# Row-chain stages and weight handling in the half passes of an interleaved convolution and MLP kernel: which is issued first in a step

## The chip, the cores and the metric

The kernel runs on one core of a Trainium2 chip. The metric is the device time of one execution of the whole program, in microseconds. The core's engines each work through a queue of their own: TensorE (PE, matmuls and transposes), VectorE (DVE), ScalarE (ACT), GpSimd (POOL) and SyncE (SP), which here issues the DMAs. An instruction that waits holds back all that stand behind it on its engine.

## The reference

Four layers, in turn of kind A and of kind B, on x of 2048 tokens (S) by 1024 channels (D), in fp32:

```
def A(q, k, v):                       # H3 convolution layer
    k_shift = causal depthwise conv of k, 4 taps
    kv = k_shift * v
    y = long causal depthwise conv of kv with ssm_k (2048 taps, by FFT) + kv * ssm_D
    return q * y
def B(x):                             # MLP, F = 3584
    h = x @ w1 + b1
    h = max(h, 0) ** 2
    return h @ w2 + b2
x = A_q
x = x + A(layernorm(x), A_k, A_v)
x = x + B(layernorm(x))
x = x + A(layernorm(x), A_k, A_v)
x = x + B(layernorm(x))
```

## The kernel before

**Tiling.** The tokens are cut into 4 blocks of 512, each of 4 tiles of 128. The MLP of one layer on one block is a unit; there are eight, in the order `ORDER = [(0,0), (1,0), (0,1), (0,2), (0,3), (1,1), (1,3), (1,2)]` (MLP layer, block). The fifth and sixth, and the seventh and eighth, are computed jointly and are not touched here. An fp32 product is made of three matmuls on split operands (`mm3`, L391 to L394): high by high, high by low, low by high. The convolution is computed by matmuls, too, and its work is spread between the steps of the MLP.

**Steps.** A unit is a list of steps. A step "m1" multiplies one 128 x 512 piece of w1 with the block's transposed, split rows (`xh`, `xl`), and adds into a PSUM bank; two such steps make 128 hidden channels, and `relu2` (L1627, L1628, L1630 on ACT, L1635 on DVE) follows. A step "m2" multiplies by a piece of w2. Mostly a step works on all 512 tokens. In a half pass it works on tiles 0 and 1 alone, or on 2 and 3 (128 x 256 matmuls). There are half passes in "m1" at the start of the first unit (4 groups of hidden channels, two steps each, on each half) and at the start of the second unit (6 groups: 12 half steps on tiles 0 and 1, then 12 on 2 and 3); the steps of the latter stand behind the last "m2" steps of the first unit, since both units work on block 0. Half steps of kind "m1" have the phase "x".

**Row chain.** Between the first two units the rows of block 0 go through the convolution layer of the second pair: the MLP result is added (`evict1`, L1737), normalised, multiplied by the convolution's y and added to the residual (`rows`, L1730 on ACT; L1720, L1722, L1724 on DVE), normalised again (L1763 on ACT, L1765 on DVE), transposed on PE (L1774) and split into `xh` (L1782 on ACT) and `xl` (L1783 on DVE). It runs on two tiles at a time, in eleven stages; the reciprocal square root is a row of short DVE instructions (L809 to L813). The stages of tiles 2 and 3 run under the half steps on tiles 0 and 1 of the second unit. Each stage has a due step, counted from the end of the half in question (the table `CHAIN`, L93); when a step comes, all stages due are issued. Other work waits in the same list (`lag`) for its due step: `relu2`, the loads of the residual rows (`load_acc`, L1796, four of 512 KB), the broadcast load of b2 (`load_b2`, L1801, 512 KB into a `px` tile) and its additions on POOL (`add_b2`, L1805). Two shorter lists, `soon` and `behind`, are emptied ahead of and behind it.

**Weights.** `w_advance(s, w)` (L1161) moves three pointers ahead of step s with weight w. It loads a raw 256 KB piece up to 9 weights ahead into one of eight `wr` rows (L1129, L1132); casts it to a high half in a `whl` or `jr` buffer (L1142, on ACT); and subtracts to make the low half (L1150). A piece that was split before can be stored (`w_store`, L1158, to a DRAM tile `wd_m...`) and loaded again later as a pair of 512 KB (L1138), which needs neither cast nor subtraction. In phase "x" the low halves go to POOL three times of four and else to DVE (`WLO`), and the pointers for cast and low half run one and two weights farther.

**Order within a step.** The loop issues `soon`, then `lag` and `w_advance` (in phase "x" `w_advance` first, else `lag` first), then `behind`, then the step's matmuls. It decides only the order within each engine's queue; semaphores do the rest.

Of the kernel before, what the change touches and what calls it, by code (L numbers as in the profile page):

```python
# [297 lines left out]
def tile_h3_mlp(ctx: ExitStack, tc: tile.TileContext, q, kT, vT, shk, ssmT, ssmD, w1, b1, w2, b2,  # L298
# [735 lines left out]
    phase = [""]  # L1034
# [27 lines left out]
    def from_pair(w):  # L1062
        return w not in single and split_kept(wsrc[w]) and w - first_w.get(wsrc[w], w) >= PAIR_GAP
# [4 lines left out]
    def room(w):  # L1068
        n = 3 if wsrc[w][0] == "s" and wsrc[w][1::2] not in parts else 1
        return all(len(ring) + k < RAWS or ring[k - RAWS].get("freed", now[0]) < now[0] - 1 for k in range(n))  # L1070
# [3 lines left out]
    def part_sums(g):  # L1074
        s2, s1, s3, s4, w22 = (g[j]["t"] for j in (6, 5, 7, 3, 4))
        V.tensor_sub(s3, s2, s1)
        V.tensor_add(s1, s1, w22)
        V.tensor_sub(s2, s1, s2)
        V.tensor_sub(s4, s4, s2)
        g["made"] = True  # L1080
# [32 lines left out]
    def w_load():  # L1113
        w = ptr["load"]
        ptr["load"] += 1
        if from_pair(w):
            return
        k, c, a, i = wsrc[w]
        if k == "s":
            raws[w] = load_part(c, a, i)  # L1120
            return
        raws[w] = row()
        raw = raws[w]["t"]
        if k == "t":
            while c not in made:
                next(tgen[0])
            SY.dma_start(raw, TD[c][:, T_AT[a]])
        elif k == "m1":
            SY.dma_start(raw, w1[c * FC + a, :, 4 * i:4 * i + 4])  # L1129
        else:  # L1130
            f = c * FC + i
            SY.dma_start(raw, w2[f * P:(f + 1) * P, a * 512:(a + 1) * 512])  # L1132

    def w_hi():
        n = ptr["hi"]
        t = his[n] = ml.tile([P, 2, 512], F32R, name="jr", bufs=NJ) if n in far else mw.tile([P, 2, 512], F32R, name="whl", bufs=6)
        if from_pair(n):
            SY.dma_start(t.bitcast(F32), WD[wsrc[n]])  # L1138
        else:
            while wsrc[n][0] == "s" and "made" not in parts[wsrc[n][1::2]]:  # L1140
                part_sums(pend.pop(0)[1])
            A.copy(t[:, 0], raws[n]["t"])  # L1142
        ptr["hi"] += 1

    def w_lo():
        n = ptr["lo"]
        t = wts[n] = his.pop(n)
        if not from_pair(n):
            e = WLO.get(phase[0], "V")
            ENG[e[n % len(e)]].tensor_sub(t[:, 1], raws[n]["t"], t[:, 0].bitcast(F32))  # L1150
            drop(raws.pop(n))
        ptr["lo"] += 1
# [7 lines left out]
    def w_advance(s, w):  # L1160
        n = len(wsrc)  # L1161
        now[0] = s
        while pend and pend[0][0] <= s:
            part_sums(pend.pop(0)[1])

        def free(k):
            if k >= n or past[k] is not None and last_use[past[k]] >= s:
                return False
            return not from_pair(k) or past[k] is None or last_use[past[k]] < s - 1

        def ahead(k):
            return w + (W_PAIR if k < n and from_pair(k) else W_HI) + (phase[0] == "x") + (k in deep and (FAR if from_pair(k) else FAR_HI))

        while ptr["lo"] < ptr["hi"] and ptr["lo"] <= w + W_LO + 2 * (phase[0] == "x"):
            w_lo()
        while free(ptr["hi"]) and ptr["hi"] <= ahead(ptr["hi"]) and ptr["hi"] < ptr["load"]:
            w_hi()
        while ptr["load"] < n and ptr["load"] <= w + W_LOAD and (from_pair(ptr["load"]) or room(ptr["load"])):
            w_load()
        while ptr["lo"] <= w:  # L1180
            if ptr["load"] <= ptr["hi"]:
                w_load()
            if ptr["hi"] <= ptr["lo"]:
                w_hi()
            w_lo()
# [434 lines left out]
    lag = slag  # L1620
# [502 lines left out]
    for s, (k, u, c, a, i, tts, w) in enumerate(steps):  # L2123
# [30 lines left out]
                J.j_p1_load(p6_at[s + 5])  # L2154
        soon.tick()
        phase[0] = "" if len(tts) == NT else "x" if k == "m1" else "b" if tts[0] else ""
        if phase[0] == "x":
            w_advance(s, w)
            lag.tick()
        else:  # L2160
            lag.tick()
            w_advance(s, w)
        behind.tick()
        if u in JS and s >= jb_at - 10:
            J.r_advance(s - jb_at)
# [150 lines left out]
        while todo > 0:  # L2316
            x = next(pds, 0)
# [62 lines left out]
```

## Time and profile before

| | |
|---|---|
| median of 3 runs | 2607.3 us (2605.19 to 2608.96) |
| the profiled execution | 2610.57 us, of which the span is 2608.8 us |
| PE, DVE, ACT, POOL busy | 98%, 74%, 44%, 39% of the span |
| mean granted TensorE clock | 0.995 |
| DMA | 792.83 MB, mean 304 GB/s |

A row of the timeline gives the start and the time of one group of like instructions in microseconds, engine and line, the operation with output and input, the count, and in brackets the idle time of that engine before it, with what released it. The name `SPq` is SyncE's queue. In the windows view a row is a stretch of time with its length, then the busy time of PE, PE's weight loads, DVE, ACT and POOL, then the granted clock, the share of the DMA engines that was in use, and GB/s.

### The profile page before, as it was taken

What the parts mean: (1) busy time and instruction counts of PE and PEld (TensorE: products, weight loads), DVE (VectorE), ACT (ScalarE), POOL (GpSimd) and SP (SyncE); (2) the same over time, 40 slices, a digit from 0 to 9 for tenths busy, and PEclk for the clock granted to TensorE, in tenths of its full rate; (3) what the DMA queues carried; (4) which work ended last, traced back from release to release, by engine and by line L of the source; (5) the groups of instructions that cost most, each with busy time, mean ns of one, the idle gap of its engine ahead of it and who ended that gap; (6) DMA issues with size and microseconds to landing.
All of it is one profiled execution on the core that took longest, in us unless ns stands there. A gap on an engine that the chain in (4) does not pass through costs nothing.

```text
span 2608.8 us, 36822 instructions
## 1 busy us (share of the span) xinstructions
PE 2569.1 (98%) x12184; PEld 2157.0 (83%) x12184; DVE 1925.9 (74%) x3053; ACT 1144.6 (44%) x2020; POOL 1010.7 (39%) x1194
## 2 busy tenths in 40 slices
PE   8999999999999999999999999999999999999999
PEld 8887888788887888888788888887888888888887
DVE  7877887768788787878789657886678666755553
ACT  4454344444435332344223456664434475553332
POOL 3546776366673788746888300000300000003000
PEclk9999999999999999999999999999999999999999
DMA  8799988889999999899999878999978566679682
GB/s 278 248 323 319 308 286 289 308 304 352 368 334 367 342 351 367 296 318 340 337 391 386 280 273 298 342 347 347 375 279 304 182 234 227 230 260 383 212 292 81
DMA packets 414929, 792.83 MB, mean 304 GB/s; under 512 B 47889, under 2 KB 163217, under 8 KB 414738
## 3 DMA queue, kind: packets, MB, share of 16 engines
q1 hardware_dynamic: 414738, 790.48, 86.2%
q8 instruction: 96, 1.57, 0.2%
q14 instruction: 95, 0.78, 0.1%
HBM read 583.22 MB, written 207.09 MB: 303 GB/s over the span
## 4 chain that ended last, share of the span: by engine, by line
PE 75%; DMA 13%; DVE 5%; POOL 4%; ACT 1%; issue 1%; SPq 1%; POOLq 0%; ACTq 0%; DVEq 0%
PE p L392 21%; PE p L394 21%; PE p L393 21%; DMA cg<-gd 3%; POOL cp L622 3%; PE pt L393 2%; PE pt L392 2%; PE pt L394 2%; DMA wr<-w 2%; DMA whl<-wd_m 2%; PE p L1227 2%; DMA gd<-fg 1%; DMA fx<-kT 1%; DVE sm L627 1%; PE pt L524 1%
## 5 line engine op out<-in xcount | busy, mean ns | idle before, releaser
L622 POOL TENSOR_TENSOR cp<-cx,cg 128x256 f32<-128x256 f32 (+1 forms) x864 | 676.7, 822 | 285.0 <-DVE sm L627 140.6
L2011 POOL TENSOR_TENSOR acc<-acc,px 128x512 f32<-128x512 f32 x16 | 24.9, 1571 | 884.6 <-DMA whl<-wd_m 503.4
L1150 DVE TENSOR_TENSOR whl<-wr,whl 128x512 fp32r<-128x512 f32 x385 | 297.8, 778 | 86.8 <-ACT whl L1142 79.1
L392 PE MATMUL p<-xh,whl 128*128 128x512 f32 (+1 forms) x932 | 358.3, 384 | 2.6 <-ACT rh L1630 2.3
L393 PE MATMUL p<-xl,whl 128*128 128x512 f32 (+1 forms) x932 | 354.3, 380 | 0.0
L394 PE MATMUL p<-xh,whl 128*128 128x512 f32 (+1 forms) x932 | 354.2, 380 | 0.0
L1142 ACT CAST whl<-wr 128x512 fp32r<-128x512 f32 x397 | 243.1, 618 | 173.9 <-PE p L394 72.8
L627 DVE TENSOR_REDUCE sm<-cp 128x128 f32<-128x384 f32 (+5 forms) x288 | 249.2, 874 | 41.1 <-POOL cp L622 40.0
L392 PE MATMUL p<-whl,rh 128*128 128x512 f32 x648 | 256.8, 396 | 3.1 <-ACT fg L546 2.4
L394 PE MATMUL p<-whl,rl 128*128 128x512 f32 x648 | 253.2, 391 | 0.0
L393 PE MATMUL p<-whl,rh 128*128 128x512 f32 x648 | 252.9, 390 | 0.0
L392 PEld LDWEIGHTS p<-xh,whl 128*128 128x128 f32 x932 | 176.9, 190 | 35.7 <-ACT rh L1630 2.6
L394 PEld LDWEIGHTS p<-xh,whl 128*128 128x128 f32 x932 | 176.5, 189 | 33.4
L393 PEld LDWEIGHTS p<-xl,whl 128*128 128x128 f32 x932 | 176.7, 190 | 31.6
L1627 ACT ACTIVATE wr<-p,b1t 128x512 f32<-128x512 f32 x110 | 75.8, 689 | 232.7 <-PE p L394 230.1
L1635 DVE TENSOR_TENSOR rl<-wr,rh 128x512 fp32r<-128x512 f32 x112 | 98.6, 880 | 88.5 <-ACT rh L1630 88.4
L392 PEld LDWEIGHTS p<-whl,rh 128*128 128x128 f32 x648 | 122.2, 189 | 28.8 <-ACT fg L546 2.8
L394 PEld LDWEIGHTS p<-whl,rl 128*128 128x128 f32 x648 | 121.9, 188 | 26.0
L393 PEld LDWEIGHTS p<-whl,rh 128*128 128x128 f32 x648 | 122.3, 189 | 24.0
L774 POOL TENSOR_TENSOR sm<-sm 128x256 f32<-128x256 f32 x96 | 81.9, 866 | 83.3 <-DVE sm L627 83.1
L392 PE MATMUL p<-jr,rh 128*128 128x512 f32 x248 | 98.2, 396 | 0.7 <-ACT jr L1142 0.7
L1685 DVE TENSOR_TENSOR acc<-p,acc 128x512 f32<-128x512 f32 x120 | 77.0, 682 | 28.5 <-PE p L394 28.5
(488 smaller groups left out, 6278.7 us busy)
## 6 DMA issues: line engine op xcount, KB each, us to landing
whl<-wd_m SPq DMA_DIRECT2D x231, 512.0 KB, 6.8
wr<-w SPq DMA_DIRECT2D x379, 256.0 KB, 5.6
rh<-rd SPq DMA_DIRECT2D x168, 256.0 KB, 5.5
jr<-wd_m SPq DMA_DIRECT2D x60, 512.0 KB, 6.5
rd<-acc SPq DMA_DIRECT2D x120, 256.0 KB, 3.2
wr<-td SPq DMA_DIRECT2D x112, 256.0 KB, 5.2
wd_m<-whl SPq DMA_DIRECT2D x49, 512.0 KB, 6.7
cx<-xd SPq DMA_DIRECT2D x48, 512.0 KB, 6.5
```

The lines of the kernel that those rows point to most:

```text
L392: PE.matmul(o, lh, rh, start=start, stop=False, skip_group_check=skip)
L393: PE.matmul(o, lh, rl, start=False, stop=False, skip_group_check=skip)
L394: PE.matmul(o, ll, rh, start=False, stop=stop, skip_group_check=skip)
L622: G.tensor_mul(pr[:, :, a:e].rearrange("p c i -> p i c"), xt[:, a:e], gt[:, j - a:j - e if e <= j else None:-1])
L627: V.tensor_reduce(sm[:, ty, jj], st["pr"], axis=AX.X, op=OP.add)
L774: E.tensor_add(s[:, k], s[:, k], s[:, 0])
L1142: A.copy(t[:, 0], raws[n]["t"])
L1150: ENG[e[n % len(e)]].tensor_sub(t[:, 1], raws[n]["t"], t[:, 0].bitcast(F32))
L1227: PE.matmul(o, lh, r, start=start, stop=stop)
L1627: A.activation(r, st["o"], AF.Relu, bias=b1t[:, st["f"]:st["f"] + 1])
L1635: V.tensor_sub(st["lo"], st["r"]["t"], st["hi"].bitcast(F32))
L1685: V.tensor_add(accs[tt][:, d], o, accs[tt][:, d])
```

## The change

In phase "x", too, `lag.tick()` is now called ahead of `w_advance(s, w)`, as in the other phases: stages of the row chain and other work that are due come ahead of the step's weight loads, casts and low halves in each engine's queue.

```diff
         soon.tick()
         phase[0] = "" if len(tts) == NT else "x" if k == "m1" else "b" if tts[0] else ""
-        if phase[0] == "x":
-            w_advance(s, w)
-            lag.tick()
-        else:
-            lag.tick()
-            w_advance(s, w)
+        lag.tick()
+        w_advance(s, w)
         behind.tick()
```

The order of the built program differs in two places. The first is SP's queue in the half passes of the first unit (`acc` are the residual rows, `wr` the raw weight rows, `fk` a piece of the convolution, `px` the tile for b2):

```order
 L508 DMA fk<-kd_0_81 128x256 x2
+L1796 DMA acc<-x_109 128x1024 x4
 L1129 DMA wr<-w 128x512 x4
-L1796 DMA acc<-x_109 128x1024 x4
 L1158 DMA wd_m_0_1_0_1566<-whl 128x1024
-L1132 DMA wr<-w 128x512
 L1801 DMA px<-b 128x1024
-L1132 DMA wr<-w 128x512
+L1132 DMA wr<-w 128x512 x2
```

The four loads of residual rows have moved ahead of four weight loads, and the load of b2 ahead of one. On ACT, in the same stretch, a cast (L1142) has moved behind a `relu2` triple, in two places.

The second is in the half passes of the second unit on tiles 0 and 1. On DVE, the rows there were these (`sd`, `rs`, `rt`, `nm` are the small tiles of the reciprocal square root and of the negated mean, `p` PSUM banks with the normalised rows):

```order
L801 TENSOR_SCALAR ve<-mv_5255 128x2
L1150 TENSOR_TENSOR whl<-wr,whl 128x512
L809 RECIPROCAL rs<-sd 128x2
L817 TENSOR_TENSOR rt<-rs 128x2
L818 TENSOR_TENSOR rt<-rt,ve 128x2
L812 TENSOR_SCALAR rt<-rt 128x2
```

and are now these:

```order
L809 RECIPROCAL rs<-sd 128x2
L817 TENSOR_TENSOR rt<-rs 128x2
L818 TENSOR_TENSOR rt<-rt,ve 128x2
L812 TENSOR_SCALAR rt<-rt 128x2
L813 TENSOR_TENSOR rs<-rs,rt 128x2
L1712 SCALAR_TENSOR_TENSOR nm<-mv_5255,rs 128x2
L1720 TENSOR_TENSOR p_5289<-p_5289,px 128x512
L1720 TENSOR_TENSOR p_5291<-p_5291,px 128x512
L1722 TENSOR_TENSOR acc<-acc,p_5289 128x512
L1722 TENSOR_TENSOR acc<-acc,p_5291 128x512
L1724 BN_STATS st_5288<-acc 128x6 x2
L1150 TENSOR_TENSOR whl<-wr,whl 128x512
```

The low half (L1150) has gone from ahead of the reciprocal to behind the first pair of pieces. On ACT the cast between the two pairs of L1730 has gone behind the second pair, and the next one behind the two L1763.

SP's queue in the same place (the pair `wd_m_0_1_1` is stored and loaded again shortly after):

```order
 L1158 DMA wd_m_0_1_1_5345<-whl 128x1024
 L1129 DMA wr<-w 128x512
+L1801 DMA px<-b 128x1024
 L1138 DMA whl<-wd_m_0_0_0_1506 128x1024
-L1801 DMA px<-b 128x1024
 L1138 DMA jr<-wd_m_0_1_0_1566 128x1024
 L1138 DMA jr<-wd_m_0_1_1_5345 128x1024
```

The load of b2 has moved ahead of the pair load into `whl`. PE's and POOL's queues hold the same instructions in the same order as before.

## The prediction

> **What bounds the kernel now.** I read the page first, for which engine is full.
>
> ```profile
> span 2608.8 us, 36822 instructions
> PE 2569.1 (98%) x12184; PEld 2157.0 (83%) x12184; DVE 1925.9 (74%) x3053; ACT 1144.6 (44%) x2020; POOL 1010.7 (39%) x1194
> ```
>
> TensorE (PE) is busy for 2569.1 of 2608.8 us. The change gives PE no instruction and takes none away, so it can only touch the 39.7 us in which PE is idle, make new idle time, or change the clock at which PE runs. So the question is which of PE's waits lie where the change moves something. The view of PE's waits has one at the end of the half passes in which the row chain runs (two waits of one kind, 5.1 us together, the longest 2.9), and PE's timeline shows both, with a third wait elsewhere that will serve as a comparison (the bracket is the idle time before the row and its releaser):
>
> ```profile
> PE p L1774 <- DVE xl L1783: 5.1, 2, 2.9
> 386.47 0.77 PE L392 MATMUL p<-whl,rh 128*128 128x512 f32 x1 [2.44 <-ACT fg L546]
> 495.97 1.26 PE L1774 MATMUL p<-ident,wr 128*128 128x128 f32 x8 [2.14 <-DVE xl L1783]
> 522.63 1.92 PE L1774 MATMUL p<-ident,wr 128*128 128x128 f32 x8 [2.94 <-DVE xl L1783]
> ```
>
> The row at 522.63 is the transposes of tile 3, the last of the chain; PE had been idle since 519.69. The chain of waits, followed back from there, gives what ended that idle time:
>
> ```profile
> 513.13 7.53 DMA wr<-w
> 520.75 0.62 ACT whl L1142
> 521.37 0.49 ACT xh L1782
> 521.89 0.70 DVE xl L1783
> 522.63 1.92 PE p L1774 x8
> ```
>
> So it was not the row chain's arithmetic that came last but a load of weights (issued at 513.13, landed at 520.66), because its cast stands ahead of the cast xh in ScalarE's (ACT's) queue. This matters for the change: stages of the chain that run earlier gain nothing there, unless that load lands earlier too.
>
> The third thing is the clock. The windows view (busy time of the five engines, then PEclk, DMA share, GB/s) shows it around these waits:
>
> ```profile
> 386.25:389.60 3.35, 3.13 (x8) 2.49 (x9) 3.35 (x7) 3.29 (x7) 3.35 (x5) 0.50 1.06 398
> 492.00:495.40 3.40, 1.83 (x12) 1.22 (x10) 3.33 (x7) 3.37 (x6) 1.43 (x2) 1.00 0.99 369
> 520.00:522.70 2.70, 0.07 (x1) 0.07 (x2) 0.81 (x2) 1.59 (x3) 2.70 (x3) 1.00 0.99 396
> 522.75:526.15 3.40, 3.40 (x17) 3.40 (x18) 2.05 (x4) 1.18 (x2) 3.40 (x5) 0.50 0.53 178
> ```
>
> After the 2.94 us of idle time, the clock stood at 0.50 for 3.4 us, which costs 3.4 x 0.5 = 1.7 us beside the idle time itself. The same came after the 2.44 us before 386.47; the 2.14 us before 495.97 passed without it (the matmuls behind it run at full speed). So a wait of about 2.4 us or more is worth 1.7 us on top, and one of 2.1 us is not.
>
> **The change, part by part.** In the built program the order on PE and GpSimd is what it was; on VectorE (DVE), ACT and the DMA queue of SyncE (SP), two places differ.
>
> Place A, second half passes of the first unit (128 to 160 us). No row chain runs here; what is due is four loads of acc (512 KB each), the load of b2, and two relu2 triples. The four acc loads now stand ahead of four weight loads (256 KB each).
>
> ```profile
> 134.57 1.80 SPq L1129 DMA_DIRECT2D wr<-w  x4
> 136.42 2.10 SPq L1796 DMA_DIRECT2D acc<-x  x4
> DMA to landing us min/median/max: 3.8/4.0/4.4
> DMA to landing us min/median/max: 7.2/8.5/9.8
> 141.82 1.12 ACT L1142 CAST jr<-wr 128x512 fp32r<-128x512 f32 x2
> 149.85 0.62 ACT L1142 CAST whl<-wr 128x512 fp32r<-128x512 f32 x1 [1.08 <-DMA wr<-w]
> 151.69 0.65 ACT L546 COPY fg<-pt 128x256 f32<-128x256 f32 x2 [1.22 <-DVE pt L539]
> 157.62 0.69 ACT L1627 ACTIVATE wr<-p,b1t 128x512 f32<-128x512 f32 x1 [2.33 <-PE p L394]
> 151.97 0.39 PE L392 MATMUL p<-xh,jr 128*128 128x512 f32 x1
> 172.00:176.00 4.00, 4.00 (x20) 3.31 (x19) 4.00 (x7) 1.34 (x3) 0.00 (x0) 1.00 0.82 244
> ```
>
> The weight loads are issued from 134.57 on and land after 4.0 us (first landing row), the acc loads from 136.42 on, after 7.2 to 9.8 (second). Exchanged, the weights are issued 2.1 us later and queue behind 2 MB: the first is in at about 145.3 instead of 134.6 + 3.8 = 138.4 (estimated: the last acc load is issued at 138.1 now, and 138.1 + 7.2 = 145.3 is when the queue that holds the same bytes is through with it). ACT wants to cast it at 141.82, so it is blocked for about 3.5 us, and with the queue around it is up to 3.9 us late. ACT's brackets behind that are 1.08 + 1.22 + 2.33 = 4.6 us of idle time up to 157.6, which take up 3.9. PE first uses one of these weights at 151.97; cast by about 145.9 and split about 0.8 us later, it is there with some 5 us to spare. In all the stretch to 228 us PE has no wait in its view. The delayed transfers themselves are taken up by about 175, where the DMA share is 0.82, so the queue is not full. One copy is close: a transpose at 157.4 takes a bank that DVE empties some 2 us before, out of ACT's copies. I take +0.3 us for A, with bounds of 0 and +1 as long as the cover holds. If the cover is gone, all 3.9 us reach PE, which is a rival below. A gain isn't in sight here: the acc tiles are wanted long after they land.
>
> Place B, the half passes of the second unit on tiles 0 and 1 (500 to 522 us). Here the chain's stages move.
>
> ```profile
> 503.72 0.30 ACT L803 ACTIVATE sd<-mv,epst 128x2 f32<-128x2 f32 x1 [4.84 <-DVE mv L1703]
> 504.56 0.69 DVE L1150 TENSOR_TENSOR whl<-wr,whl 128x512 fp32r<-128x512 f32 x1 [0.67 <-ACT whl L1142]
> 505.17 0.16 DVE L809 RECIPROCAL rs<-sd 128x2 f32<-128x2 f32 x1
> 507.16 1.40 DVE L1720 TENSOR_TENSOR p<-p,px 128x512 f32<-128x512 f32 x2 [0.85 <-ACT p L1730]
> 507.77 0.60 ACT L1142 CAST whl<-wr 128x512 fp32r<-128x512 f32 x1
> 512.58 0.28 PE L394 MATMUL p<-xh,whl 128*128 128x256 f32 x1
> 515.58 1.47 PE L325 MATMUL p<-ident 128*128 128x128 f32 x12
> 517.17 1.09 PE L1774 MATMUL p<-ident,wr 128*128 128x128 f32 x8
> 520.75 0.62 ACT L1142 CAST whl<-wr 128x512 fp32r<-128x512 f32 x1 [2.42 <-DMA wr<-w]
> ```
>
> The low half at 504.56 stood ahead of the reciprocal chain; it now stands behind the first pair's statistics. The reciprocal then waits only for ACT's sd (503.72 + 0.30) and starts at about 504.05, not at 505.17: the first pair of rows is 1.1 us earlier. The moved subtraction (0.6 us from start to next start) comes between the pairs, so the second pair is 0.5 us earlier. On ACT the cast at 507.77 goes behind the second pair (3.0 us for the two pairs of rows ahead of it), which brings the second pair's rows no nearer since they wait for DVE. On PE this buys almost nothing: the transposes of tile 2 at 517.17 come behind twelve transposes that only fill time (515.58, 1.47 us), and 0.5 us earlier there is 0.1 to 0.2 us at PE. What pays for it is that the moved low half is done at about 510.4 instead of 505.2, against a use by the 8th half step, whose twelve matmuls end at 512.86, at about 511.5: 1 us of room. A later step, whose cast now stands behind the normalise, can wait up to 0.45 us.
>
> What counts at B is the DMA queue, since the load at 513.13 sets the end of the wait.
>
> ```profile
> 511.28 0.32 SPq L1138 DMA_DIRECT2D whl<-wd_m  x1
> 511.69 0.38 SPq L1801 DMA_DIRECT2D px<-b  x1
> 512.18 0.85 SPq L1138 DMA_DIRECT2D jr<-wd_m  x2
> 513.13 0.42 SPq L1129 DMA_DIRECT2D wr<-w  x1
> SPq L1138 <- DMA wd_m<-whl: 4.2, 1, 4.2
> 510.00:512.00 2.00, 2.00 (x19) 2.00 (x19) 2.00 (x4) 0.67 (x1) 0.88 (x2) 1.00 0.05 18
> ```
>
> In this stretch SP waits 4.2 us for a store, ahead of the pair load at 511.28, and the DMA engines stand nearly empty (share 0.05). The load of b2 (px, 512 KB) now goes ahead of that wait: it is issued at about 507.5 and moves its bytes in the empty stretch. The pair load behind it writes a buffer that the 8th half step reads, and by the reordered subtraction it waits for that step's last matmul (512.58 + 0.28 = 512.86) where it went at 511.28: 1.7 us later. Queued behind it are the two jr loads and the decisive wr load, which goes at about 512.95 + 0.4 + 0.1 + 0.85 = 514.35 instead of 513.13. It is 1.2 us later in issue, with 512 KB less ahead of it; at the 396 GB/s of the full queue those are 1.3 us. The ends: if the queue is emptied at 396 GB/s from 512.95 and a latency like that of the first weight loads is in it, the load lands as much as 1.1 us sooner; if the whole shift of the first load passes through and only part of the 1.3 us is won back, 1.0 us later. I take -0.2, near the difference of the two amounts. So idle time of 2.94 becomes about 2.7 to 2.8 and the half clock stays: B is -0.2 us (bounds -1.1 and +1.0, and -2.8 if the wait falls under some 2.2 us and the 1.7 goes with it). PE doesn't wait again from 526 to 700, so what B gives or takes is kept.
>
> Sum: +0.3 - 0.2 = +0.1 us. The profiled execution took 2610.57 us, 2608.8 of span and 1.77 around it, 3.3 above the median of the runs shown (2607.3). By the sum it becomes 2610.7, and the median 2607.4.
>
> **The rivals.** Slower: the block of ACT at place A reaches PE. The cast that waits at 141.82 stands ahead of relu2 activations and of the convolution's copies. If one of these releases a PSUM bank that PE needs before ACT's idle time has taken the delay up (before 157.6), PE stands for up to 3.9 us, and after a wait of that length the clock is at 0.50 for a window: 3.9 + 1.7 = 5.6 us, 2612.9. For it: 4.6 us of idle time cover 3.9 by only 0.7, most of it in the last bracket, and the transpose at 157.4 is within 0.3 us of its bank. Against it: PE has no wait here now, and ACT is 44% busy. It decides from a landing about 1 us later than 145.3.
>
> Faster: the load of B lands 1.1 us or more earlier, the casts of xh come with it, and the wait goes. Its end is 2.94 + 1.7 = 4.6 us, 2602.7. Where the wait before 386.47 loses its half clock too, because every wait is shifted against the clock's windows, it is 6.3 us, 2601.0. For it: b2 now moves in an empty stretch. Against it: the pair load is held by PE for 1.7 us. The Trainium skill, "TensorE: Matmul & The Clock Gate", section "Part 1: The HAM clock gate (the "warmup" mystery)", asks for at least one whole idle window of some 3.4 us before the clock drops; by it a wait of 2.94 us would cost no clock and this rival would be worth 2.9 us only. The trace disagrees: 0.50 after 2.44 and after 2.94 us.
>
> Nothing but a shift: the load lands 1.0 us later and the wait grows to 3.9 us, one more microsecond at the same half clock, 2608.3. For it: the later issue. Against it: the 512 KB less.
>
> **How the numbers follow.** Some 0.2% (5.2 us) is about what a measurement of this kernel can tell from no change. My forecast of 2607.4 with its ends (-2.8 to +2) has 0.50, the third case 0.06; the faster rival has 0.20, of which 0.08 in the near form (4.6 us, still within 0.2%) and 0.12 in the far one; the slower one has 0.24, of which 0.02 stay under 5.2 us because only a part of the 3.9 gets through. That is 0.12 faster, 0.66 the same, 0.22 slower. The range goes from 2601.8, which leaves most of the far faster form out, to 2613.5, which holds the slower rival at 2612.9 with some room for the 1.9 us by which runs lie apart from their median.
>
> **What would show it.** Right at A: acc loads issued at 134.6, ACT's cast of jr waiting some 3.5 us for a DMA near 142, and no wait of PE up to 228. Right at B: b2 issued near 507.5, the pair load near 512.95, the reciprocal near 504.05, tile 3's transposes still behind 2 to 3 us of idle time that end with ACT's cast of a late load, and 0.50 behind them. The forecast is wrong if PE waits for ACT between 145 and 165, if the half clock at 522 is gone or stands elsewhere, or if a wait appears where neither order differs.

## The result, and the profile after

The changed kernel takes 2611.36 us (median of 19 runs, 2606.19 to 2615.66), the kernel before in 19 runs beside it 2607.3 us (2602.12 to 2613.33). The ratio is 1.0018, with a 95% interval of 1.0012 to 1.0025: slower by some 4 us, clear of no change, but inside the 0.2% that the prediction counted as the same. The profiled execution has a span of 2613.9 us against 2608.8; it is the slowest of the 19 runs, so the two profiles lie farther apart (5.1 us) than the medians.

The page after has PE as full as before:

```profile
span 2613.9 us, 36825 instructions
PE 2567.6 (98%) x12184; PEld 2155.7 (82%) x12184; DVE 1926.8 (74%) x3053; ACT 1143.8 (44%) x2020; POOL 1007.7 (39%) x1194
```

PE's busy time is even 1.5 us less; its idle time has grown from 39.7 to 46.3 us. Where it is, PE's timeline shows (after). The order on PE is the same in both kernels, so the same transposes can be set side by side:

```profile
119.67 0.66 PE L1532 MATMUL p<-ident,cp 128*128 128x128 f32 x4 [1.13 <-DVE xl L1541]
217.07 0.72 PE L492 MATMUL pt<-ident,fv 128*128 128x128 f32 x4 [1.31 <-DVE fg L554]
235.51 2.04 PE L524 MATMUL pt<-fg,yh 128*128 128x256 f32 x4 [5.06 <-DMA fg<-ssmT]
497.96 1.25 PE L1774 MATMUL p<-ident,wr 128*128 128x128 f32 x8 [2.15 <-DVE xl L1783]
527.08 1.97 PE L1774 MATMUL p<-ident,wr 128*128 128x128 f32 x8 [4.17 <-DVE xl L1783]
818.10 0.66 PE L888 MATMUL p<-ident,wr 128*128 128x128 f32 x4 [1.90 <-ACT wr L831]
```

And before (the other rows of before stand in the prediction):

```profile
119.45 0.66 PE L1532 MATMUL p<-ident,cp 128*128 128x128 f32 x4 [1.13 <-DVE xl L1541]
215.40 0.71 PE L492 MATMUL pt<-ident,fv 128*128 128x128 f32 x4
233.39 3.75 PE L524 MATMUL pt<-fg,yh 128*128 128x256 f32 x8 [4.62 <-DMA fg<-ssmT]
813.83 0.66 PE L888 MATMUL p<-ident,wr 128*128 128x128 f32 x4 [1.44 <-ACT wr L831]
```

The changed kernel is 0.2 us behind at 119, ahead of both places; 2.1 us at 235.5, behind place A; 2.0 us at 498; 4.45 us at 527, behind place B; 4.3 us at 818. So in this pair of profiles about 2 us were lost in the convolution behind A, and 2.5 us between tile 1's and tile 3's transposes at B.

At A, ACT's and SP's timelines of after (first two rows) and SP's of before (in the second fence):

```profile
145.60 1.27 ACT L1142 CAST jr<-wr 128x512 fp32r<-128x512 f32 x2 [3.39 <-DMA wr<-w]
160.09 1.42 SPq L561 DMA_DIRECT2D gd<-fg  x3
```

```profile
157.60 2.55 SPq L561 DMA_DIRECT2D gd<-fg  x3
```

ACT is held for 3.39 us by a weight load, as predicted, and the convolution's stores gd go 2.5 us later. PE has no wait there. It has one 57 us later (217.07, for DVE fg), in the same convolution, and the chain of waits of after, followed back from 235, goes through loads of the convolution and POOL:

```profile
191.64 6.02 DMA cg<-gd
197.79 2.29 POOL cp L622 x4
212.19 5.21 DMA cx<-xd
217.52 0.67 DVE sm L627
224.53 6.01 DMA fx<-kT
230.56 4.81 DMA fg<-ssmT
```

This part of the chain does not lead back to the late stores gd. In SP's timeline the delay is gone by 172, where a store of the convolution (xd) is 0.25 us later than before, about as much as PE was at 119. Seven microseconds on, a load of the convolution (cx) is 1.14 us later, behind three weight loads instead of two (before, then after):

```profile
171.93 0.36 SPq L484 DMA_DIRECT2D xd<-fx  x1
173.51 0.94 SPq L1132 DMA_DIRECT2D wr<-w  x2
177.88 1.34 SPq L723 DMA_DIRECT2D cx<-xd  x1
```

```profile
172.18 0.36 SPq L484 DMA_DIRECT2D xd<-fx  x1
173.75 1.41 SPq L1132 DMA_DIRECT2D wr<-w  x3
179.02 1.32 SPq L723 DMA_DIRECT2D cx<-xd  x1
```

So the first of the two places reaches farther than the list given with the change: behind its rows, too, weight loads have moved in SP's queue, some behind the convolution's loads fg and fk and one behind its stores kd.

At B, the chain of waits of after shows what stands ahead of tile 3's transposes, and SP's waits from 506 to 517 show why it went late:

```profile
516.29 0.13 PE p L394
516.49 0.33 SPq L1138
517.82 7.28 DMA wr<-w
525.19 0.62 ACT whl L1142
525.81 0.49 ACT xh L1782
```

```profile
SPq L1138 <- PE p L394: 4.5, 2, 2.4
SPq L1138 <- DVE whl L1150: 2.6, 1, 2.6
```

The same weight load ends the wait as before. It now stands behind a pair load that waits first for the moved low half on DVE and then for the end of the 8th half step on PE, where it waited for a store before.

The clock took part, too. Behind tile 1's transposes it is at half here, and before it was not, after a wait of the same length (2.15 and 2.14 us). The 1.7 us that a piece of half clock takes are most of the 2.5 us that B lost in this one pair of profiles, so B has to be judged over more kernels. The windows view of after:

```profile
499.70:503.00 3.30, 3.30 (x10) 2.56 (x9) 1.46 (x3) 1.17 (x3) 1.34 (x1) 0.51 0.16 43
```

### The profile page after: what moved, and what is told of

It reads as the page before. It is cut to its first block, busy times and chain, and to the rows that moved or that the text cites. A ratio compares the mean times of both kernels' runs of the same rounds, so it can differ in the third digit from the quotient of the medians.

```text
span 2613.9 us, 36825 instructions
## 1 busy us (share of the span) xinstructions
PE 2567.6 (98%) x12184; PEld 2155.7 (82%) x12184; DVE 1926.8 (74%) x3053; ACT 1143.8 (44%) x2020; POOL 1007.7 (39%) x1194
## 4 chain that ended last, share of the span: by engine, by line
PE 68%; DMA 16%; POOL 6%; DVE 5%; SPq 2%; issue 1%; ACT 1%; POOLq 0%; DVEq 0%; ACTq 0%
PE p L392 19%; PE p L394 19%; PE p L393 19%; POOL cp L622 5%; DMA cg<-gd 4%; DMA wr<-w 3%; PE pt L394 2%; PE pt L392 2%; PE pt L393 2%; PE p L1227 2%; DMA whl<-wd_m 1%; DMA xd<-fy 1%; DMA gd<-fg 1%; DMA wd_m<-jr 1%; DMA fx<-kT 1%
## 5 line engine op out<-in xcount | busy, mean ns | idle before, releaser
L622 POOL TENSOR_TENSOR cp<-cx,cg 128x256 f32<-128x256 f32 (+1 forms) x864 | 674.2, 819 | 289.1 <-DVE sm L627 142.9
L1150 DVE TENSOR_TENSOR whl<-wr,whl 128x512 fp32r<-128x512 f32 x385 | 297.2, 777 | 86.4 <-ACT whl L1142 81.0
L1142 ACT CAST whl<-wr 128x512 fp32r<-128x512 f32 x397 | 242.9, 618 | 171.6 <-DMA wr<-w 65.6
L1627 ACT ACTIVATE wr<-p,b1t 128x512 f32<-128x512 f32 x110 | 75.8, 689 | 236.6 <-PE p L394 234.0
L1150 DVE TENSOR_TENSOR jr<-wr,jr 128x512 fp32r<-128x512 f32 x108 | 91.1, 849 | 11.2 <-ACT jr L1142 10.5
```

The lines of the kernel that those rows point to most:

```text
L622: G.tensor_mul(pr[:, :, a:e].rearrange("p c i -> p i c"), xt[:, a:e], gt[:, j - a:j - e if e <= j else None:-1])
L1627: A.activation(r, st["o"], AF.Relu, bias=b1t[:, st["f"]:st["f"] + 1])
```

## The experiments

Two theories stood against each other. Mine after the result: each place costs about 2 us, A by the bytes ahead of the weight loads, B by the buffer that the pair load got. The rivals: all of it is made at one place; or it is the clock's chance. The whole-run times scatter by 2 to 3 us, so beside each ratio the table gives two stretches of the profiled execution, from the wait at 119 to tile 1's transposes (place A lies in it) and from there to the transposes near 813 (place B lies in it), and the wait ahead of tile 3's transposes, all from rows of PE's timeline like those above.

| kernel | 119 to 497, us | 497 to 813, us | wait of tile 3, us | ratio to before [95%] |
|---|---|---|---|---|
| before | 376.52 | 317.86 | 2.94 | |
| changed | 378.29 | 320.14 | 4.17 | 1.0018 [1.0012, 1.0025] |
| a_only | 378.00 | 316.12 | 1.30 | 1.0005 [0.9997, 1.0014] |
| a_acc_behind | 377.02 | 316.54 | 1.68 | 0.9998 [0.9987, 1.0009] |
| a_double | 382.36 | 316.47 | 1.58 | 1.0021 [1.0012, 1.0030] |
| b_only | 377.72 | 319.24 | 3.55 | 1.0008 [0.9999, 1.0017] |
| cast_moved | 377.32 | 318.33 | 4.58 | 1.0010 [1.0001, 1.0018] |
| b_own_buffer | 376.07 | 316.39 | 2.03 | 1.0002 [0.9990, 1.0014] |
| xh_first | 377.12 | 315.35 | 0 | 0.9996 [0.9987, 1.0005] |
| cast_moved_xh_first | 374.79 | 316.92 | 0 | 0.9999 [0.9988, 1.0011] |
| changed_xh_first | 379.44 | 314.88 | 0.46 | 0.9994 [0.9984, 1.0004] |
| own_buffer_xh_first | 377.19 | 312.76 | 0.46 | 0.9986 [0.9977, 0.9995] |

**Each place alone.** The edit of `a_only`; `b_only` has `and not u`:

```diff
-        if phase[0] == "x":
+        if phase[0] == "x" and u:
             w_advance(s, w)
             lag.tick()
```

> The changed order in the half passes of the first unit alone, the second unit's as before. Theory: the late weight loads hold ACT and with it the convolution's chain, which reaches PE first at 217 us (a wait of about 1.3 us for DVE fg) and again at the load of fg near 233: +1.9 us against the kernel before (ratio 1.0007). Rival (all of the loss is made at the second place, this delay is absorbed): 0 to +0.3 us.

> The changed order in the half passes of the second unit alone. Theory: the pair load of wd_m_0_0_0 overwrites a buffer that the 8th half step still reads, so it goes when that step ends; the weight load behind it lands about 1 us later against PE, and the wait of 2.9 us grows to about 4: +1 us (+2.5 if the clock also drops after the wait at 496 as in the changed kernel). Rival (all of the loss is made here): +4 us (1.0016). Rival (the 1.1 us that the rows gain reaches PE): 0 or below.

Measured: 2610.15 and 2612.14 us against 2607.77, ratios of 1.0005 and 1.0008; neither interval is clear of 1 by itself, and together they make 1.0013, within the interval of the changed kernel. But the interval of `b_only` reaches to 1.0017, so the times alone do not exclude that B makes nearly all of the loss. The profiles say more. `a_only` has a longer first stretch and not B's longer wait; `b_only` has the longer second stretch. At A, the three kernels in which the acc loads lead (changed, `a_only`, `changed_xh_first`) need 378.0 to 379.4 us for the first stretch; the seven that leave A alone need 374.8 to 377.7, with a mean of 376.7. That is +1.9 us, with a scatter of about 1 us in one profile. For `a_only` itself it is weak: its 378.0 us are 0.3 above the highest of the seven, and over both stretches it needs 694.1 us where the kernel before needs 694.4.

**The bytes at A.** The edit of `a_acc_behind`, on top of `a_only`, puts the four loads of acc behind `w_advance` again:

```diff
-                    lag.at(5, load_acc, accs, b)
+                    (lag if u else behind).at(5, load_acc, accs, b)
```

> The changed order in the half passes of the first unit alone, but with the four loads of acc behind the four weight loads again; the casts behind relu2 and the shifted loads behind them stay. Theory (the acc loads hold ACT by 3.4 us): ACT's cast near 141.8 no longer waits, the stores gd are issued near 157.6 instead of 160, no wait for DVE fg near 217, and the time is that of the kernel before, 0 to +0.5 us. Rival (the casts behind relu2 or the loads shifted behind the convolution's cost): as the first place alone, +1.3 us.

Measured 2608.47 us against 2608.41. ACT's cast no longer waits, and its timeline and SP's have the convolution's copies and stores nearly where they were before:

```profile
145.98 1.06 ACT L529 COPY fk<-pt 128x512 f32<-128x512 f32 x2
157.75 1.42 SPq L561 DMA_DIRECT2D gd<-fg  x3
```

PE still had a wait of 0.81 us for DVE fg near 216, against the expectation. That wait is no clear sign of A: in `a_only` it is 0.33 us, and two kernels that leave A alone have it, too (0.39 and 0.62 us, `xh_first` and `own_buffer_xh_first`). The first stretch is 377.0 us, within what unchanged kernels need, and 1.0 us below `a_only`, which is as much as the scatter. The three weight loads ahead of the late cx are here as well (SP's timeline):

```profile
172.07 0.36 SPq L484 DMA_DIRECT2D xd<-fx  x1
173.65 1.41 SPq L1132 DMA_DIRECT2D wr<-w  x3
178.80 1.52 SPq L723 DMA_DIRECT2D cx<-xd  x1
```

So the acc loads are what holds ACT and the stores gd. That A's loss goes with them is not shown: the rival, the shifted weight loads behind, stays. `a_double` asks from the other side, on top of `a_only`:

```diff
     def load_acc(accs, b):
+        if cur_u == 0:
+            for tt in range(NT):
+                SY.dma_start(dram.tile([P, D], F32, name="spare"), X1[b][:, tt])
         for tt in range(NT):
```

> The first place alone, with four more transfers of 512 KB (copies of the same residual rows to a spare DRAM tile) ahead of the four acc loads, so that twice the bytes stand ahead of the four weight loads; nothing else is added. Theory (the bytes ahead of the weight loads hold ACT, and through it the convolution's chain, whose cover is already used up): ACT's cast waits some 8 to 11 us instead of 3.2, the stores gd go 5 to 8 us later, and PE loses 3 to 8 us more than with the first place alone: ratio 1.0020 to 1.0040. Rival (the first place's loss comes from the shifted order of later loads, not from the bytes): 1.0005 to 1.0010 as for the first place alone.

Measured 2614.22 us against 2608.97, 1.0021 [1.0012, 1.0030]. ACT's timeline, SP's and PE's:

```profile
150.42 1.27 ACT L1142 CAST jr<-wr 128x512 fp32r<-128x512 f32 x2 [8.60 <-DMA wr<-w]
164.85 1.82 SPq L561 DMA_DIRECT2D gd<-fg  x3
```

```profile
161.07 0.72 PE L492 MATMUL pt<-ident,fv 128*128 128x128 f32 x4 [3.30 <-DVE fg L554]
```

ACT is held for 8.60 us instead of 3.19 in `a_only`, gd goes 4.7 us later, and PE stands 3.30 us at once, at the transpose that the prediction called close to its bank. The first stretch grows by 4.4 us. So 2 MB more ahead of the weight loads do reach PE, clear of no change, and the theory of this run holds for them. But most of the 4.4 us is made at a transpose at which neither `a_only` nor the changed kernel waits. How the 1.9 us of the changed kernel come about is not shown by this.

**The buffer at B.** `cast_moved` lets the due stage go ahead in one half step only, the fourth of the second unit:

```diff
-        if phase[0] == "x":
+        if phase[0] == "x" and (u == 0 or s - next(q for q, z in enumerate(steps) if z[1] == 1) != 3):
```

This moves one cast behind two rows on ACT. SP's queue holds the same rows in the same order, but in the built program the pair load now has the buffer of the 8th half step's weight, and with it the wait for that step; before, it had the buffer whose contents are stored shortly ahead of it. `b_own_buffer` is the complement: all of B's new order except in this step (`== 3`), and the pair load keeps its buffer.

> The kernel before with only one thing of the change: in one half step (the one in which the second pair of rows is issued) the due stage goes ahead, which moves one cast behind two rows on ACT and gives the pair load the other buffer; SP's queue is in the same order as before. Theory (the buffer decides): the pair load waits for PE until about 512.9, the wait ahead of tile 3's transposes grows from 2.9 to 4 us or more (b2 is behind it here): +1 to +2 us. Rival (the order of b2 and of the low half is what costs): 0.

> The changed order in the half passes of the second unit except in the one half step whose cast decided the buffer: b2 goes ahead of the pair load and the low half behind the first pair, as in the change, but the pair load overwrites the same buffer as before. Theory (the buffer makes all of the loss at the second place): no loss, 0 to -1 us; the pair load is issued when the store has landed, near 511.3, and the decisive weight load near 513, with b2 out of its way. Rival (b2 ahead or the low half behind costs by itself): +1 to +2 us, with a wait ahead of tile 3's transposes of 3.5 us or more.

Measured: 2610.95 us against 2607.77 (1.0010, just clear of 1) for the one cast, and 2608.82 against 2608.41 (1.0002) for all the rest. SP's waits from 506 to 517, in `cast_moved`:

```profile
SPq L1138 <- PE p L394: 6.5, 1, 6.5
```

and SP's timeline in `b_own_buffer`, where b2 went ahead, the pair load 2.8 us behind it, and the decisive wr load at 510.75, 15.9 us behind tile 1's transposes at 494.84 (in `b_only` 18.3 us, 515.67 - 497.38):

```profile
506.35 0.33 SPq L1801 DMA_DIRECT2D px<-b  x1
509.14 0.33 SPq L1138 DMA_DIRECT2D whl<-wd_m  x1
510.75 0.37 SPq L1129 DMA_DIRECT2D wr<-w  x1
```

The wait ahead of tile 3 is 3.55 to 4.58 us in the three kernels with the other buffer and 1.30 to 2.94 in the five with the old one (before, the three of A, `b_own_buffer`). The second stretch is 318.3 to 320.1 us with it and 316.1 to 317.9 without, 319.2 and 316.7 in the mean: 2.6 us. Of these, 2.2 us lie between tile 1's and tile 3's transposes (28.1 and 25.9 us in the mean). The clock's chance does not make them: outside PE's waits, half clock lies in that part in one kernel of each group (the changed kernel and `a_acc_behind`), and without these two the means are still 27.6 and 25.6 us. The loss at B is the buffer's; the low half and b2's place show none of their own.

**The cast in the way.** `xh_first` takes the late load out of the row chain, in the table of due steps of tiles 2 and 3; the same edit on `cast_moved` and on the changed kernel makes the other two:

```diff
-CHAIN = (..., (2, 3, 4, 5, 6, 6, 6, 11, 12, 13, 13))
+CHAIN = (..., (2, 3, 4, 5, 6, 6, 6, 11, 12, 11, 13))
```

> The kernel before, with tile 2's split into xh and xl due one step earlier, so that the two casts xh stand ahead of the cast that waits for the late load. Theory (the landing of that load ends the wait, the row chain does not): the wait of 2.9 us goes and the half clock behind it too: -4.6 us (0.9982), at least -2.9. Rival (the row chain comes last right behind the load): less than 1 us.

> The kernel with the one cast moved (other buffer, pair load late), and tile 2's casts xh ahead of the cast that waits for the late load. Theory (the late load hurts only since a cast that waits for it stands ahead of xh): the wait of 4.6 us in the run with the cast moved goes; 2 to 4 us faster than that, level with the run of xh first alone (ratio 0.9990 to 1.0003). Rival (the late buffer costs PE otherwise too, in the half steps behind): as slow as with the cast moved alone, 1.0010.

> The changed kernel with tile 2's casts xh ahead of the cast that waits for the late load. Theory: what the second place costs (+2 to +3 us) goes, what the first place costs stays: ratio to the kernel before 1.000 to 1.0007, no wait over 1 us ahead of tile 3's transposes. Rival (the loss is made elsewhere): 1.0018 as for the changed kernel.

Measured: 2607.21 us against 2607.77 (0.9996), 2608.85 against 2608.41 (0.9999) and 2607.38 against 2608.41 (0.9994). ACT's timeline in `cast_moved_xh_first` shows the late load as late as ever, with both casts xh of tile 2 now ahead of it:

```profile
517.80 1.06 ACT L1782 CAST xh<-p 128x512 fp32r<-128x512 f32 x2
521.85 0.62 ACT L1142 CAST whl<-wr 128x512 fp32r<-128x512 f32 x1 [2.99 <-DMA wr<-w]
522.37 1.07 ACT L1782 CAST xh<-p 128x512 fp32r<-128x512 f32 x2
```

The wait ahead of tile 3 goes in all three (0.46 us of it stays in `changed_xh_first`), and with it what the buffer cost: 0.9999 where the cast alone had 1.0010. A wait of 1.17 us for tile 3's own cast takes a part of its place in this one. In `changed_xh_first` what A costs should have stayed, 1.0000 to 1.0007, and 0.9994 is below that: its first stretch is long (379.44 us), but its time shows no loss at A. And `xh_first` on the kernel before should have won 4.6 us, or 2.9 at least, and won 0.6, with an interval from -3.4 to +1.3. In its profile the wait is gone, the half clock stands behind tile 1's wait instead, and the second stretch is 2.5 us shorter, not 4.6; the wait near 813 for ACT is 2.28 us there instead of 1.44.

**A version that beats both** takes B's order with the old buffer and the casts xh first:

> A version meant to beat both: the second place in the changed order except for the step that swaps the buffer, and tile 2's casts xh ahead of the late cast; the first place as before. Theory (PE's wait of 2 to 3 us ahead of tile 3's transposes is gone, nothing new stands in its place): 1 to 3 us faster than before, ratio 0.9988 to 0.9996. Rival (what is won there is given back at the next waits, for ACT near 813 us and for a DMA near 1297): 1.0000.

Measured 2605.67 us against 2608.97: 0.9986 [0.9977, 0.9995], 3.3 us faster than before, a little more than the 1 to 3 us expected. SP issues the late load early enough now that its cast no longer waits (ACT's timeline):

```profile
519.36 1.06 ACT L1782 CAST xh<-p 128x512 fp32r<-128x512 f32 x2
520.31 0.62 ACT L1142 CAST whl<-wr 128x512 fp32r<-128x512 f32 x1
```

## Why the prediction was right or wrong, point by point

The time lies in the range, and within the 0.2% that the most likely case named. The centre did not hold: +0.1 us was forecast and some +4 measured, beyond the +2 at which that case ended. That the change still counts as none is in part luck: the two terms of the sum missed by 1.6 and 2.8 us in the same direction, which together stays just under 5.2 us. By its own signs the working was wrong: a wait appeared at 217, where it expected none, and a half clock stood behind tile 1's transposes as well.

**Place A, +0.3 us, bounds 0 and +1.** Right: no wait of PE for ACT between 145 and 165, the issue of the acc loads at 134.7, ACT's wait of 3.4 us (3.5 predicted). The idle time of ACT did take the delay up (L1627 at 157.86 instead of 157.62), and SP was level again at 172. Wrong: that nothing is left of it then. The term is +1.9 us by the stretches, three profiles against seven. The prediction followed the acc loads, ACT's queue and PE's weights; it did not follow the weight loads that had moved behind the convolution's loads. From 179 on the convolution's loads are late, and POOL, which waits for one of them, starts its row L622 at 197.79 instead of 196.75; PE waits at 217. The absence of a PE wait before 228 in the old trace was read as room. Whether the acc loads or the shifted weight loads make the 1.9 us was not separated by a run and stays open. The slower rival did not happen in the changed kernel: no wait for a PSUM bank before 157.6 and no half clock there. Its bank is what comes when the block is larger (`a_double`, 3.30 us at 161).

**Place B, -0.2 us, bounds -1.1 and +1.0.** Right: the cast that waits for the wr load sets the end of the wait, the chain's gain of 1.1 us buys nothing on PE, and the pair load goes when the 8th half step ends. Even the issue of the wr load came as predicted: 18.3 us behind tile 1's transposes in `b_only`, 18.4 by the prediction (514.35 - 495.97); in the changed kernel it is 19.9 (517.82 - 497.96), with the half clock between. Wrong was the reason given for the later pair load, the reordered subtraction: `cast_moved` leaves the subtraction where it was, and its pair load waits for that step all the same; `b_own_buffer` moves it, and its pair load does not. It is the other buffer. Wrong, too, that the 512 KB taken out from ahead of the wr load win back 1.3 us: it took 7.53 us from issue to landing before, 7.28 after and 6.66 in `b_only`. Over all kernels it is 7.1 to 7.7 us with b2 just ahead and 6.7 to 7.5 without, 0.4 us less in the mean, so most of the later issue passed through. And the comparison started from one profile: with the old buffer the load is issued 15.9 to 17.5 us behind tile 1's transposes in five kernels, and before's 17.2 is near the late end of it, as its wait of 2.94 us is the longest of the five. The term is +2.6 us by the stretches, above the upper bound of 1.0. The rival "nothing but a shift", with a chance of 0.06, came nearest at B: the wait grew by 1.2 us in the changed kernel, at the same half clock.

**The clock.** The wait of tile 3 kept its half clock, as forecast. But "some 2.4 us or more is worth 1.7, one of 2.1 is not" fell: in ten of the twelve profiles tile 1's wait is 2.14 or 2.15 us, and the half clock follows it in three (the changed kernel, `xh_first`, `a_acc_behind`) and not in seven. The Trainium skill, "TensorE: Matmul & The Clock Gate", section "Part 1: The HAM clock gate (the "warmup" mystery)", has the clock drop only after a whole idle window of some 3.4 us; these waits of 2.15 us, and those of 2.4 and 2.9, disagree. What decides between waits of equal length is in the traces. In each of the twelve profiles the half clock starts on a grid: all its starts lie whole multiples of 3.413 us apart (before, at 386.2, 413.5 and 522.7: 8 and 32 steps). The windows view by such steps around tile 1's wait, of after and then of before:

```profile
496.10:499.51 3.41, 1.55 (x10) 1.30 (x11) 2.61 (x5) 2.10 (x5) 2.35 (x2) 1.00 0.94 365
499.51:502.92 3.41, 3.41 (x9) 2.67 (x8) 1.65 (x3) 1.36 (x3) 1.34 (x1) 0.50 0.14 37
```

```profile
492.00:495.41 3.41, 1.83 (x12) 1.22 (x10) 3.34 (x7) 3.37 (x6) 1.44 (x2) 1.00 0.99 370
495.41:498.82 3.41, 2.85 (x16) 2.37 (x17) 2.64 (x5) 2.15 (x4) 1.06 (x1) 1.00 0.58 229
```

In the changed kernel PE idles for 1.9 us of one step (3.41 - 1.55), and the next step runs at half; before, the wait falls on two steps, of which the emptier has 1.6 us of idle time. Over the ten waits, the emptier step has 1.9 to 2.15 us of idle time in the three that the half clock followed and 1.3 to 1.8 in the seven others. Even a wait of 3.06 us ahead of 388.56 in the changed kernel, split into 1.3 and 1.7, passed at full clock. One piece does not fit: at 524.8 in `cast_moved_xh_first` the half clock follows a step with 1.5 us.

The price of 1.7 us on top fell, too. From tile 3's transposes to the row near 813, `a_only` without any half clock needs 291.1 us, the kernel before with one piece 291.2, and `cast_moved` and `b_only` with two 290.0 and 292.3. The wait near 813 is 2.22 us in `a_only` and 1.44, 0.32 and 1.50 in the others, so it can take up part of it. That would fit the 0.6 us that `xh_first` won; it was not tried by itself.

**The faster rival** lives in the last experiment only: what was won there is 3.3 us, below its 4.6.

## What to carry to other kernels

When an instruction moves ahead of an allocation, look at which buffer the moved or following load gets, not only at the queue's order: one cast moved by two rows turned a load's wait for a store into a wait for a later matmul step. Compare the whole order of a queue and not only the first rows that differ: here weight loads had moved farther back as well, and whether they or the loads of residual rows cost the time at A is open. And a work item that is needed soon should not stand behind one that waits for a transfer: with the casts xh ahead, the late load cost nothing that the measurement could tell from zero (0.9999).

## What the runs showed of the hardware

The half clock came in pieces of one length, 3.4 us with a loss of 1.71 us, or two of them in a row, on a grid of 3.413 us within each execution. It followed tile 1's wait where PE had idled for 1.9 us or more of one step of that grid, and not where the same 2.15 us were split over two steps with at most 1.8 us in either. How many pieces there are differs from one profile to the next: by the granted clock, 7.4 to 14.4 us were lost in the twelve profiles, 12.2 before and 14.4 after. That is as large as the effect studied here, and it is why the two stretches say more than one pair of spans. The 256 KB load at B took 7.1 to 7.7 us to land with 2 MB issued just ahead of it and 6.7 to 7.5 with 1.5 MB.
